# Down projection of an adaLN block: the first token pair with ten instead of eight pairs of K tiles in seven products

## Chip, core and metric

The kernel runs on one core of one Trainium2 chip. The metric is the device time of one execution in microseconds (us), the median of several runs. The engines of the core run side by side, each with its own queue of instructions, and wait for each other by semaphores: PE (TensorE, the matmuls), DVE (VectorE), ACT (ScalarE), POOL (GpSimd) and SP (SyncE, which issues nearly all DMAs here). K is the dimension that a matmul sums over; a K tile is 128 of it.

## What is computed

A transformer block of 2048 tokens and width 1024: a layer norm with modulation, linear attention, a second modulated layer norm, and a gated feed-forward network (FFN) of inner width 3584. The part that matters here is the last line of `_B_ref`, the product of the 2048 x 3584 gated values with `w_down`, and the residual sum around it.

```
def _B_ref(x, w_gate, w_up, w_down):
    return _gelu(x @ w_gate) * (x @ w_up) @ w_down
...
h = _layernorm(x, axis=-1) * (1 + cb) + sb
x = x + gb * _B_ref(h, B_w_gate, B_w_up, B_w_down)
return x
```

## The kernel before

**Stages.** Layer norm and attention take up to about 240 us. Then the FFN runs as 28 units (`unit`, L1514), 14 for each half of the tokens; a unit computes 256 of the 3584 gated values and stores them to DRAM (`y_store`, L1506) from one of three output tiles YS. From about 600 us the down projection runs, in eight token pairs of two chunks of 128 tokens. This change concerns the first of them, pair 0, which begins inside the last unit.

**Seven products.** The gate, up and down matrices are multiplied by the Strassen-Winograd scheme. For the down projection the two token chunks of a pair make two rows of blocks, the two halves of 512 output columns two columns of blocks, and two neighbouring K tiles the inner index. Eight block products become seven: P1 and P2 take the plain bf16 operands, P5, P6, P7, P3 and P4 take sums of blocks, held as fp32r. A product is one 128 x 128 by 128 x 512 matmul for each pair of K tiles (`d_prod`, L1667). The 28 K tiles make 14 such pairs, numbered j. Pairs 1 to 7 use all 14. Pair 0 uses the products for j = 0 to 7 (`NJP`, L67); its other twelve K tiles are multiplied plainly, twelve matmuls for each of its four output parts (`down`, L1603).

**Operands.** The weights come in seven loads of four K tiles, wd 0 to 6 (`wd_dma`, L1383), so load q serves j = 2q and 2q + 1. From each load `d_t` (L1620) makes five T operands: T0, T1, T2 on DVE, T3 a copy on ACT, and T4 on DVE, which overwrites the right half of the load itself, so that this half can no longer be used plainly. P5 uses S0 and T0, P6 S1 and T1, P7 S2 and T2, P3 S3 and T3, P4 S4 and T4. The S operands are sums of a pair's y blocks (`d_s`, L1647): S0 to S3 on DVE, S4 a copy on ACT, each in two halves, j = 0 to 6 and the rest. They share two buffers: S0, S2, S4 the one, S1, S3 the other, in alternation from pair to pair, so S2 can be written when P5 has read S0, and S3 when P6 has read S1.

**PSUM banks of pair 0.** P1 and P2 sum in bank 0. ACT copies P1 into bank 2 (`d_cp`), P6 adds to it, ACT copies that into bank 1, P7 and later P4 add to bank 2. P5 stands alone in bank 3; ACT copies it to the tile DE (`d_ecp`). DVE adds DE to bank 1 (`d_add(1, 1)`) and writes bank 2 plus DE into bank 3 (`d_add(3, 2)`). P3 adds to bank 1. The plain parts 0 to 3 add to banks 0, 1, 2 and 3.

**Order.** In this stage every engine's order is the program order of the Python code; nothing reorders it. `d_pair0` (L1716) issues the products and plain parts of pair 0; P1 was already issued by `d_first` inside the last unit, ahead of that unit's own product P4 (list at L1864). After each step `hook0` (L1874) issues other work: the T sums of the later loads, S sums, evacuations (`evac`, L1588, two DVE steps and a store), and reloads of y for pair 1 (`y_in`, L1584), which can only start where pair 0 has finished with the y it replaces. In this list a number k from 1 to 7 is product Pk, 0 is the plain part 0, and 11, 12, 13 are the plain parts 1, 2, 3.

**Memory.** Many tiles lie in memory that earlier ones have left. Each `OFF_DT` entry (L72) gives the places of T0 to T3 of a load. Load 4's T0 and T1 lie where an operand of the last unit's P4 lies, T2 where another operand of that P4 lies, and T3 lies in the output tile YS0, which the last unit stores. A tracker derives every wait from these places.

Of the kernel before, what the change touches and what calls it, by code (L numbers as in the profile page):

```python
# [33 lines left out]
OFF_HT = OFF_XALL + NCH * HP * 2  # L34
# [15 lines left out]
OFF_GAB = OFF_CONST  # L50
# [13 lines left out]
OFF_KVT = OFF_GUH + 2048  # L64
OFF_YS = [OFF_YT + 32768 + i * 4096 for i in range(3)]
NDJ = NFC // 2
NJP = (8,) + (NDJ,) * 7  # L67
NSJ = NDJ // 2
YRB = NDJ * 2 * P * 2
WDQ = [OFF_R3, OFF_R3 + 8192, OFF_R3 + 16384, OFF_WS, OFF_HT + 16384, OFF_WS + 8192, OFF_WS + 16384]  # L70
# [1 line left out]
OFF_DT = (tuple(OFF_XALL + i * 4096 for i in range(4)), tuple(OFF_XALL + i * 4096 for i in range(4, 8)),  # L72
          (OFF_HT, OFF_HT + 4096, OFF_GUH, OFF_GUH + 4096),
          (OFF_YS[1], OFF_TMP + 8192, OFF_TMP + 4096, OFF_YS[2]),
          (OFF_HT + 8192, OFF_HT + 12288, OFF_R3 + 24576, OFF_YS[0]),
          (OFF_GAB, OFF_ROW, OFF_YT, OFF_YT + 4096),
          tuple(OFF_YT + 16384 + i * 4096 for i in range(4)))
OFF_YA = (OFF_HT + 24576, OFF_YT + 45056)
OFF_SB = [(OFF_YT + 45056 + YRB, OFF_YT + 8192), (OFF_SMALL + 2048, OFF_YT + 8192 + NSJ * 512)]
# [251 lines left out]
def bass_adaLN_cond__linear_attn_block__geglu_ffn__prompt_kernel(  # L331
# [18 lines left out]
    with ExitStack() as es:  # L350
# [1032 lines left out]
        def wd_dma(q):  # L1383
            f0, f1 = 4 * q, 4 * q + 4
            sch.dma(Q, lambda e: e.dma_start(WDT[q][:], wd_v[:, f0:f1, :]), wr=[t_ for fc in range(f0, f1) for t_ in r_wd(fc)], note=f"wd{q}")
# [194 lines left out]
        def x_in(i, *ns):  # L1580
            for n in ns:
                sch.dma(Q, lambda e, n=n: e.dma_start(XQ[n][:], scr_x[:, 2 * i + n // 2, n % 2 * 512:n % 2 * 512 + 512]), wr=r_xq(n), deps=[x_st[i // 2]], note=f"xq{i}.{n}")

        def y_in(i, r, j0=0, j1=NDJ):  # L1584
            sch.dma(Q, lambda e: e.dma_start(YA[r][:, j0:j1, :], scr_y[2 * i + r, :, j0:j1, :]), wr=[(OFF_YA[r] + j0 * 512, OFF_YA[r] + j1 * 512, f"ya{r}")],
                    deps=[y_st[u] for u in range(i // CPG * NFP, (i // CPG + 1) * NFP)], note=f"{'ya' if j0 == 0 else 'yt'}{i}.{r}")

        def evac(c_, k, b, c0, c1):  # L1588
            n = 2 * (c_ % 2) + k
            sch.op(V, lambda e: e.tensor_tensor(PS(b), PS(b), GBB[:, c0:c1], ALU.mult), prd=pr(b), pwr=pr(b), rd=R_GBB, note=f"x2a c{c_}.{k}")  # L1590
            sch.op(V, lambda e: e.tensor_tensor(XQ[n][:, :], PS(b), XQ[n][:, :], ALU.add), prd=pr(b), rd=r_xq(n), wr=r_xq(n), note=f"x2b c{c_}.{k}")
            sch.dma(Q, lambda e: e.dma_start(out_v[:, c_, c0:c1], XQ[n][:, :]), rd=r_xq(n), note=f"out{c_}.{k}")
# [27 lines left out]
        def d_t(i, q):  # L1620
            j0, j1 = 0, 2
            w = WDT[q][:, 2 * j0:2 * j1, :].rearrange("p (j r) d -> p j r d", r=2)
            b = lambda r, cc: (w[:, :, r, cc * 512:(cc + 1) * 512], r_wh(q, r, cc, f"wd{q}", j0, j1))
            t32 = lambda k: (dt_ap(q, k, j0, j1)[0].bitcast(f32), dt_ap(q, k, j0, j1)[1])
            dst, wr = dt_ap(q, i, j0, j1)
            if i == 3:
                src, rd = b(1, 1)
                sch.op(A, lambda e: e.activation(dst, src, ACTF.Copy), rd=rd, wr=wr, note=f"dtcp {q}")
                return
            (in0, r0), (in1, r1) = ((b(0, 1), b(0, 0)), (b(1, 1), t32(0)), (b(1, 1), b(0, 1)), None, (b(1, 0), t32(1)))[i]  # L1630
            if i == 4:
                in0, in1 = (t_.rearrange("p j (h c) -> p j h c", h=2) for t_ in (in0, in1))
            sch.op(V, lambda e: e.tensor_tensor(dst, in0, in1, ALU.subtract), rd=r0 + r1, wr=wr, note=f"dtsum {q}.{i}")

        def nj(ca):
            return NJP[ca // 2]

# [9 lines left out]
        def d_s(ca, i, hs=(0, 1)):  # L1647
            cb, n = ca + 1, nj(ca)
            for j0, j1 in (((0, min(n, NSJ)), (NSJ, n))[h] for h in hs):
                if j0 >= j1:  # L1650
                    continue
                dst, wr = ds_ap(ca, i, j0, j1)
                if i == 4:
                    src, rd = y_ap(cb, 1, j0, j1)
                    sch.op(A, lambda e, dst=dst, src=src: e.activation(dst, src, ACTF.Copy), rd=rd, wr=wr, note=f"dscp {cb}")
                    continue
                s_ = lambda k: (ds_ap(ca, k, j0, j1)[0].bitcast(f32), ds_ap(ca, k, j0, j1)[1])
                (in0, r0), (in1, r1), op = ((y_ap(cb, 0, j0, j1), y_ap(cb, 1, j0, j1), ALU.add), (s_(0), y_ap(ca, 0, j0, j1), ALU.subtract),
                                            (y_ap(ca, 0, j0, j1), y_ap(cb, 0, j0, j1), ALU.subtract), (y_ap(ca, 1, j0, j1), s_(1), ALU.subtract))[i]
                sch.op(V, lambda e, dst=dst, in0=in0, in1=in1, op=op: e.tensor_tensor(dst, in0, in1, op), rd=r0 + r1, wr=wr, note=f"dssum{i} {cb}")  # L1660
# [39 lines left out]
        def parts_of(i):  # L1700
            return tuple((2 * i + n // 2, n % 2, i % 2 * 4 + n, n % 2 * 512, n % 2 * 512 + 512) for n in range(4))
# [4 lines left out]
        def d_add(dst, src):  # L1706
            sch.op(V, lambda e: e.tensor_tensor(PS(dst), PS(src), DE[:, :], ALU.add), prd=pr(src), rd=R_DE, pwr=pr(dst), note="dpadd")

        def d_ecp(b):
            sch.op(A, lambda e: e.activation(DE[:, :], PS(b), ACTF.Copy), prd=pr(b), wr=R_DE, note="descp")  # L1710
# [4 lines left out]

        def d_pair0(hook):  # L1716
            parts = parts_of(0)
            for k in (2, 6, 5, 0, 7, 3, 13, 11, 12, 4):
                n = k - 10 if k > 10 else k
                if k in (0, 11, 12, 13):  # L1720
                    down(*parts[n], list(range(2 * nj(0), NFC)), n != 2, True)
                    hook(k)
                    continue
                d_prod(0, 0, k)
                if k == 6:
                    d_cp(1, 2, "ducp")
                elif k == 5:
                    d_ecp(3)
                    d_add(1, 1)
                elif k == 7:  # L1730
                    d_add(3, 2)
                hook(k)
# [128 lines left out]
        for u in range(2 * NFP):  # L1861
            if u == 0:
                unit(u, ORD0)
            elif u == 2 * NFP - 1:  # L1864
                unit(u, (1, lambda: (d_t(0, 3), d_s(0, 0, (0,)), d_s(0, 1, (0,))), 2, lambda: (wd_dma(4), wd_dma(5)), 6, 5, 7,
                         lambda: (d_t(1, 3), d_s(0, 0, (1,)), d_s(0, 1, (1,))), 3, lambda: (wd_dma(6), x_in(0, 0, 1, 2, 3)), d_first, lambda: (d_t(2, 3), d_t(3, 3)), 4))
            else:
                a = ACTS.get(u, ((), ()))
                unit(u, (1, 2, lat(DMAS.get(u, nop), DVES.get(u, nop), *a[0]), 6, 5, lat(*a[1]), 7, 3, 4))
            if u == 1:  # L1870
                mark.append(sch.n)
        held[0]()
        held[0] = None
        def hook0(k):  # L1874
            if k == 2:
                d_t(0, 4)
            elif k == 6:
                d_s(0, 3)
                d_t(0, 5)
            elif k == 5:  # L1880
                d_s(0, 2)
                y_in(1, 0, 0, nj(0))
            elif k == 0:
                evac(*parts_of(0)[0])
            elif k == 7:
                d_s(0, 4)
                y_in(1, 1, 0, nj(0))
                d_t(4, 3)
                d_t(0, 6)
            elif k == 3:  # L1890
                d_t(1, 4)
                d_t(1, 5)
                d_t(3, 4)
            elif k == 13:
                d_t(1, 6)
                d_s(2, 0, (0,))
                d_t(3, 5)
            elif k == 11:
                d_t(2, 4)
                d_t(3, 6)  # L1900
            elif k == 12:
                for r in range(2):
                    y_in(1, r, nj(0), NDJ)
                evac(*parts_of(0)[3])
            elif k == 4:
                x_in(1, 0, 3)
                d_s(2, 1, (0,))
                d_s(2, 0, (1,))
                d_s(2, 1, (1,))

        def hooks(i):
            def hook(k):
                more = i + 1 < 2 * CPG
                if i == 1:
                    if k in (6, 2):
                        n = 1 if k == 6 else 2
                        evac(*parts_of(0)[n])
                        x_in(1, n)
                    if k in (6, 7, 2):
                        d_t(4, {6: 4, 7: 5, 2: 6}[k])  # L1920
                else:
                    if k == 5:
                        x_in(i, 1, 2)
                    if not more and k in (5, 6):
                        for q in {5: (0, 1), 6: (2,)}[k]:
                            t_gb(q)
                if more and k in (1, 4):
                    x_in(i + 1, 3 if k == 1 else 0)
            return hook
# [82 lines left out]
```

## Time and profile before

| | us |
|---|---|
| median of 3 runs | 782.14 (781.69 to 782.68) |
| profiled execution | 781.62 |
| its span, first to last instruction | 779.8 |
| PE busy in the span | 773.0 |
| DVE busy | 647.4 |
| ACT busy | 377.3 |
| first matmul of pair 0 starts at | 597.64 |
| opening product of pair 1 starts at | 622.60 |
| pair 1, opening products to opening products | 635.18 to 657.22 |
| pair 2, the same | 657.22 to 679.19 |

All times in the trace count from the span's first instruction. The granted clock of TensorE was 1.00 throughout. Matmuls overlap in the array, so the row of a group tells its pitch by the number in it, not by the length of one. In a row of the timeline the square brackets give how long the engine had been idle before it and what released it. The row of a DMA shows when SP issued it; its landing, when the semaphore tells that all of it has arrived, is a number of its own.

### The profile page before, as it was taken

To read this page: it belongs to the slowest core of one execution; us is meant where nothing else is said; L and a number is where in the kernel's file an instruction comes from. 1 tells how busy PE (TensorE), PEld (TensorE's weight loads), DVE (VectorE), ACT (ScalarE), POOL (GpSimd) and SP (SyncE) were. 2 spreads that over 40 slices of the span, in tenths; PEclk is the share of its full clock that TensorE was granted. 3 is DMA by queue.
4 is the path that set the end of the run, shared out by engine and by line. 5 is a ranking of instruction groups with operands and counts; after the bars stand their busy time and mean duration, and the time that the engine had idled before them with its cause. 6 is when DMAs were issued, how large, how long until landed. Compare 5 with 4: busy or idle time off the path is not lost.

```text
span 779.8 us, 10832 instructions
## 1 busy us (share of the span) xinstructions
PE 773.0 (99%) x3883; PEld 496.9 (64%) x3883; DVE 647.4 (83%) x970; ACT 377.3 (48%) x635; POOL 49.2 (6%) x126
## 2 busy tenths in 40 slices
PE   8999999999999999999999999999999999999998
PEld 4444445666445667767676767667676567777766
DVE  6699988897898878787989888898989888667668
ACT  2497743242484487877755555555555211101111
POOL 2031300000331011100000000000000000000000
PEclk9999999999999999999999999999999999999999
DMA  9789749949996258967353865535357334443341
GB/s 290 250 169 251 157 94 221 258 125 203 209 271 182 82 147 204 237 169 215 104 140 110 261 203 168 149 96 162 98 146 223 111 123 142 137 148 98 132 143 54
DMA packets 196940, 130.22 MB, mean 167 GB/s; under 512 B 69516, under 2 KB 182420, under 8 KB 195864
## 3 DMA queue, kind: packets, MB, share of 16 engines
q1 hardware_dynamic: 196872, 129.55, 62.2%
q8 instruction: 30, 0.49, 0.3%
q14 instruction: 22, 0.18, 0.1%
q10 hardware_dynamic: 16, 0.00, 0.0%
HBM read 92.55 MB, written 23.35 MB: 149 GB/s over the span
## 4 chain that ended last, share of the span: by engine, by line
PE 96%; SPq 2%; DMA 1%; DVE 0%; issue 0%; DVEq 0%
PE ps_all L1472 45%; PE ps_all L1684 21%; PE ps_all L895 7%; PE ps_all L1292 7%; PE ps_all L934 7%; PE ps_all L880 6%; PE ps_all L1607 1%; SPq L598 1%; DMA wmq<-in_w_mod_dram 1%; SPq L603 1%; PE ps_all L913 0%; PE ps_all L1203 0%; PE ps_all L1246 0%; SPq L592 0%; PE ps_all L766 0%; PE ps_all L840 0%
## 5 line engine op out<-in xcount | busy, mean ns | idle before, releaser
L1472 PE MATMUL ps_all<-ss,tp 128*128 128x512 f32 x896 | 214.3, 396 | 0.0
L1472 PEld LDWEIGHTS ps_all<-ss,tp 128*128 128x128 f32 x896 | 168.2, 188 | 37.8 <-DVE ss L1427 0.3
L1472 PE MATMUL ps_all<-h2a,wt 128*128 128x512 bf16 x448 | 101.6, 380 | 0.0
L1684 PE MATMUL ps_all<-dt,sb 128*128 128x512 f32 x424 | 101.1, 394 | 0.0
L1495 ACT ACTIVATE ge<-ps_all 128x512 f32<-128x512 f32 x112 | 64.2, 597 | 73.8 <-DVE ps_all L1483 62.1
L1684 PEld LDWEIGHTS ps_all<-dt,sb 128*128 128x128 f32 x424 | 79.5, 188 | 17.9 <-DVE sb L1660 0.5
L1490 DVE TENSOR_TENSOR ps_all<-ps_all,es 128x512 f32<-128x512 f32 x54 | 37.6, 699 | 49.6 <-ACT es L1480 49.3
L1502 DVE TENSOR_TENSOR ys<-ge,ps_all 128x512 bf16<-128x512 f32 x112 | 74.5, 684 | 3.4 <-PE ps_all L1684 0.5
L1472 PEld LDWEIGHTS ps_all<-h2a,wt 128*128 128x128 bf16 x448 | 37.9, 97 | 57.3 <-ACT ps_all L1477 17.0
L1447 DVE TENSOR_TENSOR tp<-wt,tp 128x1024 fp32r<-128x1024 bf16 x56 | 68.3, 1220 | 0.0
L1447 DVE TENSOR_TENSOR tp<-wt 128x1024 fp32r<-128x1024 bf16 x56 | 68.2, 1218 | 0.0
L880 PE MATMUL ps_all<-wk,h1T 128*128 128x512 bf16 x248 | 56.8, 379 | 0.5 <-DVE h1T L724 0.5
L934 PE MATMUL ps_all<-h1T,wq 128*128 128x512 bf16 x256 | 56.7, 379 | 0.0
L1292 PE MATMUL ps_all<-w,pq 128*128 128x512 bf16 x256 | 56.4, 379 | 0.0
L1472 PE MATMUL ps_all<-ar,tp 128*128 128x512 f32 x224 | 55.5, 390 | 0.0
L869 ACT ACTIVATE eb<-ps_all 128x512 f32<-128x512 f32 x64 | 36.5, 595 | 38.2 <-PE ps_all L880 16.3
L1710 ACT ACTIVATE de<-ps_all 128x512 f32<-128x512 f32 x14 | 8.4, 599 | 90.2 <-PE ps_all L1684 90.2
L1684 PE MATMUL ps_all<-wd,ya 128*128 128x512 bf16 x212 | 47.7, 380 | 0.0
L1472 PEld LDWEIGHTS ps_all<-ar,tp 128*128 128x128 f32 x224 | 42.0, 188 | 8.8
L1477 ACT ACTIVATE ps_all<-ps_all 128x512 f32<-128x512 f32 x56 | 32.6, 583 | 30.7 <-PE ps_all L1472 30.7
L934 PEld LDWEIGHTS ps_all<-h1T,wq 128*128 128x128 bf16 x256 | 25.0, 98 | 30.0
L1292 PEld LDWEIGHTS ps_all<-w,pq 128*128 128x128 bf16 x256 | 24.7, 98 | 30.2 <-issue 1.1
(141 smaller groups left out, 992.2 us busy)
## 6 DMA issues: line engine op xcount, KB each, us to landing
wt<-in_B_w_gate_dram SPq DMA_DIRECT2D x28, 512.0 KB, 4.0
wt<-in_B_w_up_dram SPq DMA_DIRECT2D x28, 512.0 KB, 5.2
scr_y<-ys SPq DMA_DIRECT2D x28, 512.0 KB, 3.2
ya<-scr_y SPq DMA_DIRECT2D x14, 896.0 KB, 5.0
rb<-scr_rd SPq DMA_DIRECT2D x32, 256.0 KB, 6.4
wd<-in_B_w_down_dram SPq DMA_DIRECT2D x7, 1024.0 KB, 7.3
wmst<-in_w_mod_dram SPq DMA_DIRECT2D x6, 1024.0 KB, 5.8
wmq<-in_w_mod_dram SPq DMA_DIRECT2D x8, 512.0 KB, 6.9
```

Source lines behind the costliest of these rows:

```text
L869: sch.op(A, lambda e: e.activation(EB[i][:, :], PS(bank), ACTF.Exp), prd=pr(bank), wr=rng, note=f"{note}.exp")
L880: o = sch.op(T, lambda e, dc=dc: e.matmul(PS(bank), H1[sg][:, ci, dc, :], W_[:, dc, jg * 512:(jg + 1) * 512], start=(dc == 0), stop=(dc == ...
L895: o = sch.op(T, lambda e, c_=c_: e.matmul(PS(bank, 0, n), PK[c_][:, g * P:(g + 1) * P], xrow(c_, o_, o_ + n), start=(c_ == 0), stop=(c_ == ...
L934: o = sch.op(T, lambda e, dc=dc: e.matmul(PS(b), WQ[:, dc, qc * P:(qc + 1) * P], H1[sg][:, :, dc, :], start=(dc == 0), stop=(dc == NDC - 1 ...
L1292: last[half] = sch.op(T, lambda e, g=g, half=half: e.matmul(PS(b0 + half), PQ[sg][:, g, ci * P:(ci + 1) * P], W2[:, g, half * 512:(half + ...
L1447: sch.op(V, lambda e: e.tensor_tensor(TP[k][:], in0, in1 if k in (0, 2) else in1[:], ALU.subtract), rd=r0 + r1, wr=r_tp(k), deps=[x1_ops[7 ...
L1472: o = sch.op(T, lambda e, l_=l_, r_=r_, dc=dc: e.matmul(PS(b), l_, r_, start=fresh and dc == 0, stop=dc == ND2 - 1, skip_group_check=True) ...
L1477: sch.op(A, lambda e: e.activation(PS(BB + t), PS(BA + t), ACTF.Copy), prd=pr(BA + t), pwr=pr(BB + t), note="pcp")
L1490: sch.op(V, lambda e: e.tensor_tensor(PS(BC + t), PS(BC + t), ES[t][:, :], ALU.add), prd=pr(BC + t), rd=r_2k(OFF_ES[t], f"es{t}"), pwr=pr( ...
L1495: sch.op(A, lambda e: e.activation(GE[i][:, :], PS(b), ACTF.Gelu_apprx_tanh), prd=pr(b), wr=r_2k(OFF_GE[i], f"ge{i}"), note="gelu")
L1502: sch.op(V, lambda e: e.tensor_tensor(YS[s_][:, 2 * h:2 * h + 2, t, :], q(GE[i][:, :]), q(PS(b + 1)), ALU.mult), rd=r_2k(OFF_GE[i], f"ge{i ...
L1684: o = sch.op(T, lambda e, l_=l_, r_=r_, j=j, dst=dst: e.matmul(dst, l_[:, 0, :], r_, start=(k in (1, 5) or k == 7 and 0 < ca < 4 * CPG - 2 ...
```

## The change

Pair 0 takes ten pairs of K tiles in seven products and eight K tiles plainly. Product P5 goes ahead of P6. For this the five T operands of load 4 are made earlier: T0 inside the last unit, ahead of its last output product; T1 and T3 behind P2; T2 behind P5; T4, which was made in pair 1, behind P7. S2 is now issued ahead of S3, S3 behind part 0's matmuls, and the first two sums of loads 5 and 6 move back by one step. T0 and T1 of load 4 now lie where an operand of the last unit's P5 lay, and T2 and T3 of load 5 take their old places.

```
-NJP = (8,) + (NDJ,) * 7
+NJP = (10,) + (NDJ,) * 7
...
-          (OFF_HT + 8192, OFF_HT + 12288, OFF_R3 + 24576, OFF_YS[0]),
-          (OFF_GAB, OFF_ROW, OFF_YT, OFF_YT + 4096),
+          (OFF_YT, OFF_YT + 4096, OFF_R3 + 24576, OFF_YS[0]),
+          (OFF_GAB, OFF_ROW, OFF_HT + 8192, OFF_HT + 12288),
...
         def d_pair0(hook):
-            for k in (2, 6, 5, 0, 7, 3, 13, 11, 12, 4):
+            for k in (2, 5, 6, 0, 7, 3, 13, 11, 12, 4):
...
                 d_prod(0, 0, k)
-                if k == 6:
+                if k == 5:
+                    d_ecp(3)
+                elif k == 6:
                     d_cp(1, 2, "ducp")
-                elif k == 5:
-                    d_ecp(3)
+                    hook(k)
                     d_add(1, 1)
+                    continue
...
             elif u == 2 * NFP - 1:
-                         ... d_first, lambda: (d_t(2, 3), d_t(3, 3)), 4))
+                         ... d_first, lambda: (d_t(2, 3), d_t(3, 3), d_t(0, 4)), 4))
...
         def hook0(k):
             if k == 2:
-                d_t(0, 4)
-            elif k == 6:
-                d_s(0, 3)
-                d_t(0, 5)
+                d_t(1, 4)
+                d_t(3, 4)
             elif k == 5:
                 d_s(0, 2)
+                d_t(2, 4)
+            elif k == 6:
                 y_in(1, 0, 0, nj(0))
             elif k == 0:
+                d_s(0, 3)
                 evac(*parts_of(0)[0])
             elif k == 7:
                 d_s(0, 4)
                 y_in(1, 1, 0, nj(0))
                 d_t(4, 3)
+                d_t(4, 4)
+                d_t(0, 5)
+            elif k == 3:
                 d_t(0, 6)
-            elif k == 3:
-                d_t(1, 4)
                 d_t(1, 5)
-                d_t(3, 4)
             elif k == 13:
                 d_t(1, 6)
                 d_s(2, 0, (0,))
                 d_t(3, 5)
             elif k == 11:
-                d_t(2, 4)
                 d_t(3, 6)
...
         def hooks(i):
-                    if k in (6, 7, 2):
-                        d_t(4, {6: 4, 7: 5, 2: 6}[k])
+                    if k in (7, 2):
+                        d_t(4, {7: 5, 2: 6}[k])
```

More of the change, by code (lines that the diff above doesn't have):

```diff
@@ L1865, in bass_adaLN_cond__linear_attn_block__geglu_ffn__prompt_kernel @@
                 unit(u, (1, lambda: (d_t(0, 3), d_s(0, 0, (0,)), d_s(0, 1, (0,))), 2, lambda: (wd_dma(4), wd_dma(5)), 6, 5, 7,
-                         lambda: (d_t(1, 3), d_s(0, 0, (1,)), d_s(0, 1, (1,))), 3, lambda: (wd_dma(6), x_in(0, 0, 1, 2, 3)), d_first, lambda: (d_t(2, 3), d_t(3, 3)), 4))
+                         lambda: (d_t(1, 3), d_s(0, 0, (1,)), d_s(0, 1, (1,))), 3, lambda: (wd_dma(6), x_in(0, 0, 1, 2, 3)), d_first, lambda: (d_t(2, 3), d_t(3, 3), d_t(0, 4)), 4))
             else:
```

## Prediction

> **What bounds the kernel now.** I read the page first: how busy the engines are and the chain of waits that ended last.
>
> ```profile
> span 779.8 us, 10832 instructions
> ...
> PE 773.0 (99%) x3883; PEld 496.9 (64%) x3883; DVE 647.4 (83%) x970; ACT 377.3 (48%) x635; POOL 49.2 (6%) x126
> ...
> PE 96%; SPq 2%; DMA 1%; DVE 0%; issue 0%; DVEq 0%
> ```
>
> TensorE is the bound from end to end. A change gains only by issuing fewer or shorter matmuls, or by removing a stall of PE; it loses only where it makes PE wait. So I need the pitch of the two kinds of matmul, and PE's present stalls. The timeline of a later, undisturbed pair gives the pitch (columns: start, length, engine, line, operation, count).
>
> ```profile
> 657.22 6.22 PE L1684 MATMUL ps_all<-wd,ya 128*128 128x512 bf16 x28
> ...
> 663.08 3.57 PE L1684 MATMUL ps_all<-dt,sb 128*128 128x512 f32 x14
> ...
> 679.19 6.22 PE L1684 MATMUL ps_all<-wd,ya 128*128 128x512 bf16 x28
> ```
>
> A single matmul is shown as 0.38 us long, but they are pipelined: 28 plain ones take 6.22, so the pitch is (6.22 - 0.38)/27 = **0.2163 us**. From 657.22 to 679.19 lie 28 of these and 70 sum products (f32 operands): (21.97 - 28 x 0.2163)/70 = **0.2274 us**. A sum product costs 0.011 us more than a plain one. Next, PE's timeline over the first pair.
>
> ```profile
> 597.64 1.90 PE L1684 MATMUL ps_all<-wd,ya 128*128 128x512 bf16 x8
> 599.19 2.19 PE L1472 MATMUL ps_all<-ar,tp 128*128 128x512 f32 x8
> 601.22 1.90 PE L1684 MATMUL ps_all<-wd,ya 128*128 128x512 bf16 x8
> 602.77 4.00 PE L1684 MATMUL ps_all<-dt,sb 128*128 128x512 f32 x16
> 606.61 2.76 PE L1607 MATMUL ps_all<-wd,ya 128*128 128x512 bf16 x12
> 609.18 3.93 PE L1684 MATMUL ps_all<-dt,sb 128*128 128x512 f32 x16
> 612.95 7.94 PE L1607 MATMUL ps_all<-wd,ya 128*128 128x512 bf16 x36
> 620.54 2.21 PE L1684 MATMUL ps_all<-dh,sb 128*128 128x512 f32 x8
> 622.60 3.19 PE L1684 MATMUL ps_all<-wd,ya 128*128 128x512 bf16 x14
> ```
>
> From the first product (597.64) to pair 1's opening product (622.60) are 24.96 us. In it are 16 + 48 = 64 plain and 40 + 8 sum matmuls (8 belong to the last FFN unit): 64 x 0.2163 + 48 x 0.2274 = 24.76. So only 0.20 is stall. Stretch by stretch: 606.61 to 612.95 is 6.34 against 12 x 0.2163 + 16 x 0.2274 = 6.23, a stall of 0.10; the other three stretches lose 0.02 to 0.04 each, 0.10 together, at the changes of kind. The 0.10 is P7's wait for S2, named by the weight load's row, first below.
>
> ```profile
> 609.18 3.50 PEld L1684 LDWEIGHTS ps_all<-dt,sb 128*128 128x128 f32 x16 [0.30 <-DVE sb L1660]
> ...
> 647.56 2.59 PEld L1684 LDWEIGHTS ps_all<-dt,sb 128*128 128x128 f32 x12 [0.19 <-DVE sb L1660]
> ```
>
> The second is pair 2's S0, late behind pair 1's sums on DVE. It costs 0.07: pair 1, from 635.18 to 657.22, lasts 22.04 against the next pair's 21.97.
>
> **The change, part by part.**
>
> *PE's work.* Seven products over ten pairs of K tiles are 70 matmuls (20 plain, 50 sum), where there were 56 (16, 40); four parts over eight K tiles are 32, where there were 48. 104 become 102. Plain 64 to 52 saves 12 x 0.2163 = 2.60, sum 40 to 50 costs 10 x 0.2274 = 2.27: **-0.32 us**. That is the whole certain gain: each pair of K tiles moved swaps 8 plain matmuls for 7, five of them dearer.
>
> *The new course of PE*, by these pitches from 597.64: P1 to 599.80, the unit's P4 to 601.62, P2 to 603.78, P5 to 606.06, P6 to 608.33, part 0 to 610.06, P7 to 612.34, P3 to 614.61, three parts to 619.80, P4 to 622.08. Against it I lay each operand's arrival.
>
> *Third S-sums.* The second halves of S0 and S1 cover three j instead of one. DVE rows: 1.09 us for 896 columns, 0.28 for 128; by the line between them 384 columns take 0.55, so +0.27 each. The output product behind them (599.35) and all that follows on DVE slip by 0.54. Nothing on PE waits for these: S0 is first used at 603.78. Cost 0.
>
> *Fifth load's sums.* T0 of load 4 now stands on DVE ahead of the last output product: 599.94 + 0.54 is T2 of load 3, one step of 1.14 later (sums follow at 1.14: 3.49 for three) T0 runs 601.62 to 602.84; P5 wants it at its ninth matmul, 605.6. Its operand, load 4, was issued at 590.55 and lands 6.6 us later (597.1), also ahead of P1's ninth matmul (599.4). T1 runs from about 603.4 to 604.6, P6 wants it at 607.9. S2's first half starts when P5 has read that half of S0, near 605.6; S2 is done by 607.2; T2 by 608.4, wanted by P7 at 611.9. S2's first half is there three microseconds before P7 at 610.06: **the 0.10 stall goes**. Cost 0 as long as DVE keeps this lead.
>
> *The output store and the scalar copy.* This is the one new wait. T3 of load 4 (a copy on ACT, in the buffer of the last output tile) moves from behind P3 to right behind P2, and has to wait until the last store of that tile has landed. Behind it on ACT stand P5's copy to DE and the copy of bank 2 to bank 1; P7 may not add to bank 2 before that copy, and DVE's sum in bank 1 waits for it. The page's DMA issues, SP's timeline and the DMA issues of that one moment give the last store: issued 602.41 and 4.9 us to landing, where the median of the 28 stores is 3.2.
>
> ```profile
> scr_y<-ys SPq DMA_DIRECT2D x28, 512.0 KB, 3.2
> ...
> 602.41 0.37 SPq L1508 DMA_DIRECT2D scr_y<-ys  x1
> ...
> scr_y<-ys SPq DMA_DIRECT2D x1, 512.0 KB, 4.9
> ```
>
> After the change the output product is not at 601.64 but behind T0, at 602.76, so the store is issued near 603.53. With 3.2 it lands at 606.7, with 4.9 at 608.4. T3 then takes 1.05, the copy to DE 0.60, the copy of the bank 0.58 (rows of 600.07, 606.81, 604.99), some 0.1 overlapped each: bank 2 is free 2.2 us after landing, at 608.9 but not before P6 has ended (608.5) plus 0.6, so 609.15; or at 610.6. P7 is due at 610.06. So the cost lies between **0 and +0.55**. I take 0, since the 4.9 row shared the DMA engines with load 6 and four residual loads issued at 597.88 to 599.97, whose queue will have drained 1.1 us further when the store starts.
>
> The Trainium skill, page "DMA: Bandwidth & Descriptors", section on the anatomy of one DMA, fits a transfer (one that GpSimd issues) as 2.0 us plus its bytes over 436 GB/s: for this store an estimate of 3.2 us, which the median row matches and the 4.9 row doesn't. By the rule the sum stays as it is, by that row it gives back 0.55.
>
> *Reloads of y.* SP's order is kept. The first reload (640 KB instead of 512) is freed by S2 at 607.2 instead of 609.39; the second by S4 and S3, near 614.1 instead of 612.41, and with the 3.6 us of its row lands near 618. DVE uses them for pair 1's S0 only at 620.2. The tails (256 KB instead of 384) go after the last plain part, 620.05 and 620.45 instead of 620.76 and 621.17; at the 3.4 us of their row they land by 623.9. The opening product wants its eleventh pair at 622.08 + 10 x 0.2163 = 624.2. Cost 0.
>
> *DVE to the end of the pair.* Bank 1's sum at 609.2, S3 to 611.4 (P3 at 612.34), evacuation of part 0 to 612.8, bank 3's sum to 613.5 (its plain part at 614.61), then six T-sums to 620.2 where there were five sums, of which one is T4 of load 4, brought forward from pair 1. Pair 1's S0 is complete by 624.9, wanted at 625.1 (first half, done 621.2) and 626.7. With T4 gone from pair 1, its DVE work ends 1.1 us sooner and the 0.07 wait of pair 2 goes: **-0.07**.
>
> **Sum**: -0.32 - 0.10 - 0.07 = -0.49. The profiled execution goes from its 779.8 (781.62 with what lies around the span) to 779.3; the median of the runs shown, 782.14, to **781.65**.
>
> **Rivals.**
>
> *B, the store eats the gain.* It again takes 4.9 us, P7 waits 0.55, and the sum is +0.06: 782.2. For it: the same load 6 and residual loads go ahead of the store. Against it: the shortest and the median of the 28 stores are both 3.2, and what was ahead has 1.1 us more.
> Here the order on ACT decides: in this trace T3 of load 4 ran only at 612.23, behind S4's copy, which itself waited 3.76 for PE, although its buffer was free at 607.3. The Trainium skill, "TensorE: Matmul & The Clock Gate", section "Architectural detail", says that ScalarE's queue is strictly in order; the trace agrees.
>
> *C, slower: the queue on ACT.* The same copy as in B, but with a store so late that P7 stands still. From a landing at about 607.9 each microsecond goes into P7's start; from 608.4 (4.9 after issue) the whole is slower than before. The far row is load 5 with 8.6 us to landing: 612.1, bank 2 free at 614.3, P7 4.2 late, net +3.7: 785.9. Against it: that was 1 MB, and behind another.
>
> *D, the trade yields half on PE.* If sum matmuls ran at the spacing that half the saving needs, (2.60 - 0.16)/10 = 0.244, for example with DVE and PE contending, only -0.33 would be left: 781.8. The undisturbed pairs speak against it.
>
> **Numbers.** Forecast 0.66, B 0.23, C 0.05, D 0.06. A measurement of this kernel tells about 0.2% (1.56 us) from no change; forecast, B and D all lie inside. Their extremes are 781.65 and 782.2; the runs shown scatter by -0.45 and +0.54 about their median, so the range is 780.9 to 782.8, with C outside. Slower 0.05; faster 0.03, since no more than 0.49 can be found in PE; within, 0.92.
>
> **What would show it.** The line of seven products: 432, 108 and 216 matmuls instead of 424, 106 and 212; the plain line 32 instead of 48. Pair 1's opening product at 622.2 instead of 622.60. No wait of DVE's S-sums ahead of P7, nor at pair 2. The copy of bank 2 (ACT, line of 604.99) ending before 610.0; if P7 starts late and that copy is its releaser, B or C. I am wrong altogether if PE stalls over 0.3 us anywhere from 597 to 660.

## The result and the profile after

| | before | changed |
|---|---|---|
| median of 22 runs each, us | 782.34 (781.57 to 784.58) | 781.52 (780.37 to 782.60) |
| ratio, 95% interval | | 0.9986 (0.9980 to 0.9993) |
| the same kernels, two later comparisons (11 runs of the changed one each) | | 0.9998 (0.9989 to 1.0007), 0.9993 (0.9984 to 1.0002) |
| profiled span, us | 779.8 | 779.7 |
| pair 0's first product to pair 1's opening product | 24.96 | 24.51 |
| pair 0's first product to pair 2's P2 | 59.58 | 59.09 |

The median is 781.52 where 781.65 was forecast. The change gains a little, and less than one comparison of this kernel can size: the three ratios mean gains of 1.1, 0.2 and 0.5 us. The trace sizes it better. From pair 0's first product to pair 2's P2 it shows -0.49 us, and the two later traces of the changed kernel give 59.09 again. A later pair runs P5, P6, P7, P2, the next pair's P1, P3, P4; so each row of 28 plain matmuls, as those at 635.18 and 657.22 before, is a pair's P2 and then the next pair's opening product, and the start of pair 2's P2 is what the expectation of ten_again below calls pair 2's opening. The two spans differ by only 0.1 because the start of pair 0, ahead of which nothing was changed, fell at 597.64 before and at 598.15 in the changed kernel's profile; in its later traces it fell at 597.77 and 597.99.

The page of the changed kernel: span, busy time, and the two groups of its products with sums and its plain products.

```profile
span 779.7 us, 10826 instructions
...
PE 773.1 (99%) x3881; PEld 498.7 (64%) x3881; DVE 648.1 (83%) x970; ACT 377.0 (48%) x635; POOL 49.7 (6%) x126
...
PE 96%; SPq 2%; DMA 1%; DVE 0%; issue 0%; DVEq 0%
...
L1684 PE MATMUL ps_all<-dt,sb 128*128 128x512 f32 x432 | 103.0, 394 | 0.0
...
L1684 PE MATMUL ps_all<-wd,ya 128*128 128x512 bf16 x216 | 48.4, 380 | 0.0
```

Two matmuls fewer (x3883 to x3881), and the counts 432 and 216. PE is the bound as before. Its timeline over pair 0, in the same columns as before:

```profile
598.15 2.33 PE L1684 MATMUL ps_all<-wd,ya 128*128 128x512 bf16 x10
600.13 2.18 PE L1472 MATMUL ps_all<-ar,tp 128*128 128x512 f32 x8
602.15 2.33 PE L1684 MATMUL ps_all<-wd,ya 128*128 128x512 bf16 x10
604.13 4.90 PE L1684 MATMUL ps_all<-dt,sb 128*128 128x512 f32 x20
608.87 1.90 PE L1607 MATMUL ps_all<-wd,ya 128*128 128x512 bf16 x8
610.42 4.91 PE L1684 MATMUL ps_all<-dt,sb 128*128 128x512 f32 x20
615.17 5.35 PE L1607 MATMUL ps_all<-wd,ya 128*128 128x512 bf16 x24
620.17 2.64 PE L1684 MATMUL ps_all<-dh,sb 128*128 128x512 f32 x10
622.66 3.19 PE L1684 MATMUL ps_all<-wd,ya 128*128 128x512 bf16 x14
```

52 plain and 58 sum matmuls at the pitches 0.2163 and 0.2274 make 24.44; the stretch is 24.51, so 0.07 of stall is left where there was 0.20. The weight loads ahead of P7 and of pair 2's P5, which reads S0, no longer wait for DVE.

```profile
610.39 4.51 PEld L1684 LDWEIGHTS ps_all<-dt,sb 128*128 128x128 f32 x20
...
647.49 9.48 PEld L1684 LDWEIGHTS ps_all<-dt,sb 128*128 128x128 f32 x42
```

ACT's timeline shows the one new wait:

```profile
607.96 1.06 ACT L1628 ACTIVATE dt<-wd 128x1024 fp32r<-128x1024 bf16 x1 [5.41 <-DMA scr_y<-ys]
608.92 0.58 ACT L1710 ACTIVATE de<-ps_all 128x512 f32<-128x512 f32 x1
609.40 0.59 ACT L1704 ACTIVATE ps_all<-ps_all 128x512 f32<-128x512 f32 x1
```

ACT stands 5.41 us for the last store, then makes T3 of load 4 and the two bank copies. The second ends at 609.99, and P7 starts at 610.42: 0.43 us to spare. So the question for the experiments is what covered the trade and what this wait would cost.

### The profile page after: what moved, and what is told of

It is laid out like the page before. It is cut to its first block, busy times and chain, and to the rows that moved or that the text cites. A ratio compares the mean times of both kernels' runs of the same rounds, so it can differ in the third digit from the quotient of the medians.

```text
span 779.7 us, 10826 instructions
## 1 busy us (share of the span) xinstructions
PE 773.1 (99%) x3881; PEld 498.7 (64%) x3881; DVE 648.1 (83%) x970; ACT 377.0 (48%) x635; POOL 49.7 (6%) x126
## 4 chain that ended last, share of the span: by engine, by line
PE 96%; SPq 2%; DMA 1%; DVE 0%; issue 0%; DVEq 0%
PE ps_all L1472 45%; PE ps_all L1684 22%; PE ps_all L895 7%; PE ps_all L1292 7%; PE ps_all L934 7%; PE ps_all L880 6%; SPq L598 1%; DMA wmq<-in_w_mod_dram 1%; PE ps_all L1607 1%; SPq L603 1%; PE ps_all L913 0%; PE ps_all L1203 0%; PE ps_all L1246 0%; SPq L592 0%; PE ps_all L840 0%
## 5 line engine op out<-in xcount | busy, mean ns | idle before, releaser
L1684 PE MATMUL ps_all<-dt,sb 128*128 128x512 f32 x432 | 103.0, 394 | 0.0
L1684 PEld LDWEIGHTS ps_all<-dt,sb 128*128 128x128 f32 x432 | 81.2, 188 | 17.9
```

The source lines that it names most:

```text
L1684: o = sch.op(T, lambda e, l_=l_, r_=r_, j=j, dst=dst: e.matmul(dst, l_[:, 0, :], r_, start=(k in (1, 5) or k == 7 and 0 < ca < 4 * CPG - 2 ...
```

## The experiments

In some of these traces the first matmul record of a group of plain ones is missing. So the table measures from the end of the last FFN unit's P3 (0.2274, one pitch, after its last matmul starts) to the start of pair 1's first sum product, whose record all have, and from there to the start of the last matmul. Times in us, each from one profiled execution.

| kernel | pair 0 | to the last matmul | ratio of the runs, where timed |
|---|---|---|---|
| before | 27.81 | 150.99 | |
| changed, three traces | 27.35 | 150.80 | above |
| order_only | 28.50 | 150.90 | 1.0008 (0.9998 to 1.0018) |
| s2_first | 27.75 | 150.85 | 1.0001 (0.9992 to 1.0010) |
| order_copy_behind | 27.75 | 150.83 | |
| copy_behind | 27.35 | 150.81 | |
| store_sooner | 27.35 | 150.81 | |
| store_later | 27.57 | 150.80 | |
| two_more_copies | 29.14 | 150.81 | |
| twelve_pairs | 27.36 | 151.02 | 0.9990 (0.9981 to 0.9999) |
| unit_first | 27.08 | 151.48 | 0.9998 (0.9989 to 1.0007) |
| unit_first_2 | 27.11 | 151.33 | 0.9987 (0.9978 to 0.9996) |

**The order alone.** The changed kernel with eight pairs:

```
-NJP = (10,) + (NDJ,) * 7
+NJP = (8,) + (NDJ,) * 7
...
             elif k == 7:
-                d_t(4, 4)
...
-                    if k in (7, 2):
-                        d_t(4, {7: 5, 2: 6}[k])
+                    if k in (6, 7, 2):
+                        d_t(4, {6: 4, 7: 5, 2: 6}[k])
```

> The change's order and its early sums of load 4, but eight pairs of K tiles in products and twelve K tiles plain as before (T4 of load 4 stays in pair 1). Theory, the gain is the trade of matmuls (-0.32 us) plus two short waits: from pair 0's first product to pair 1's opening product 24.86 us (before 24.96, changed 24.51), the wait ahead of P7 gone, time 0.1 to 0.2 us under before. Rival, the order brings the gain: 24.5 to 24.6 us and a time like the changed kernel's, 0.5 to 1.1 us under before.

Neither came true: the stretch grew to 25.65, 0.70 longer than before. ACT's and PE's rows say where.

```profile
607.78 1.06 ACT L1628 ACTIVATE dt<-wd 128x1024 fp32r<-128x1024 bf16 x1 [6.03 <-DMA scr_y<-ys]
608.74 0.58 ACT L1710 ACTIVATE de<-ps_all 128x512 f32<-128x512 f32 x1
609.22 0.59 ACT L1704 ACTIVATE ps_all<-ps_all 128x512 f32<-128x512 f32 x1
```

```profile
606.75 2.76 PE L1607 MATMUL ps_all<-wd,ya 128*128 128x512 bf16 x12
609.95 3.88 PE L1684 MATMUL ps_all<-dt,sb 128*128 128x512 f32 x16 [0.44 <-ACT ps_all L1704]
```

P7 waited for ACT's copy of bank 2, which ended at 609.81, and started at 609.95, 12.17 us after pair 0's first product (597.78). In the next kernel, where nothing holds it up, it starts 11.39 after it, 0.78 sooner. The store landed 4.6 us after its issue here. Behind P7 another weight load, at 613.79, waited 0.39 for DVE's sum in bank 3, which had slipped with it. This is the forecast's rival B, in a kernel with less cover: with ten pairs P7 starts 12.27 us after pair 0's first product (610.42 less 598.15). Those 0.88 us, the longer products ahead of P7, are what the changed kernel gives ACT; by the count of matmuls they are 0.91.

**The same with the copy out of the way.** In that kernel T3 of load 4 goes behind the copy of bank 2 on ACT:

```
             if k == 2:
                 d_t(1, 4)
-                d_t(3, 4)
...
             elif k == 6:
                 y_in(1, 0, 0, nj(0))
+                d_t(3, 4)
```

> The kernel with the change's order and eight pairs (order_only), with T3 of load 4 moved on ACT behind the copy of bank 2. Theory, order_only lost its 0.70 us only to ACT's wait for the last store: without it the stretch from pair 0's first product to pair 1's first sum product is 27.7 us (before 27.80, order_only 28.50), and the copy stands well ahead of P7. Rival, DVE's order (S3 behind part 0, the sum in bank 3 late) cost a part of it: 28.0 to 28.5 us.

```profile
609.08 4.03 PE L1684 MATMUL ps_all<-dt,sb 128*128 128x512 f32 x16
```

Measured 27.75, as the theory said: moving one copy gives back 0.76 us, all that order_only lost and 0.06 more. DVE's order cost nothing by itself. Against copy_behind below (27.35), in which T3 stands in the same place, this also isolates the trade of matmuls, ten pairs against eight in nearly the same order (T4 of load 4 stands elsewhere): -0.39, of which 0.32 is the count of matmuls by their pitch. The other 0.07 is spread in bits of 0.01 to 0.03 over the stretches and is not settled.

**S2 first, in the kernel before.** The one edit lets S2 go to DVE ahead of the sum in bank 1:

```
                 elif k == 5:
                     d_ecp(3)
+                    hook(k)
                     d_add(1, 1)
+                    continue
```

> The kernel before with one edit: S2 is issued on DVE ahead of the sum in bank 1, which waits for the copy to DE. Theory, P7's wait in the kernel before came from DVE's order, not from PE's: S2 is done near 608.2 and the stretch to pair 1's opening product falls from 24.96 to 24.86 us, with no other change. Rival, P7 waits for S2 because P5 comes late behind P6: the wait stays and the stretch stays 24.96 us.

```profile
609.24 2.72 PEld L1684 LDWEIGHTS ps_all<-dt,sb 128*128 128x128 f32 x12
```

The weight load ahead of P7 no longer waits for S2, and the stretch falls from 24.96 to 24.90: the direction of the theory, 0.06 of the 0.10. So P7's old wait came from DVE's order and not from P6 standing ahead of P5; order_copy_behind, in which P5 does go first, has the same 24.90. The other 0.04 is not explained. The run times can't tell a thing of this size.

**How much ACT can bear.** First the changed kernel with `d_t(3, 4)` written three times in `hook0`, k == 2.

> The changed kernel with the copy T3 of load 4 made three times, so that two more copies of 0.95 us stand on ACT between the landing of the last store and the copies of the banks. Theory, ACT's order is the only new tight place and its lead ahead of P7 is 0.4 us (the copy of bank 2 ended at 609.99, P7 started at 610.42): P7 starts 1.5 us late and the stretch from pair 0's first product to pair 1's opening product is 26.0 us instead of 24.51. Rival, the copies hide behind PE's queue or behind part 0's plain matmuls: 24.5 us.

```profile
607.45 3.24 ACT L1628 ACTIVATE dt<-wd 128x1024 fp32r<-128x1024 bf16 x3 [5.41 <-DMA scr_y<-ys]
610.60 0.58 ACT L1710 ACTIVATE de<-ps_all 128x512 f32<-128x512 f32 x1
611.08 0.59 ACT L1704 ACTIVATE ps_all<-ps_all 128x512 f32<-128x512 f32 x1
```

```profile
608.36 1.90 PE L1607 MATMUL ps_all<-wd,ya 128*128 128x512 bf16 x7
611.81 4.57 PE L1684 MATMUL ps_all<-dt,sb 128*128 128x512 f32 x19 [1.54 <-ACT ps_all L1704]
```

The three copies, which write the same place, took 3.24, so each further one 1.09 and not the 0.95 of copies to different places: 2.18 more. The stretch grew by 1.79, so 0.39 was hidden: the lead read from the trace (0.43). The theory holds, its number was low by the longer copies. What went past that lead, PE lost.

Then the opposite: in the changed kernel the copy T3 goes behind the copy of bank 2, with the edit of order_copy_behind.

> The changed kernel with T3 of load 4 issued on ACT behind the copy of bank 2, so that nothing ahead of P7 waits for the store. Theory, the lead of the bank's copy over P7 grows from 0.4 to over 0.9 us, and PE's stretch stays 24.5 us, since the wait cost nothing. Rival, the store's wait does cost PE: the stretch falls below 24.4 us.

27.35, unchanged. The bank's copy ended at 609.56 for a P7 at 610.33, a lead of 0.77 rather than over 0.9, since it is then P6's end that sets it. In the changed kernel the wait for the store costs nothing, but by a margin of only 0.4 us.

**When the store is issued.** T0 of load 4 behind the last output product:

```
-  ... d_first, lambda: (d_t(2, 3), d_t(3, 3), d_t(0, 4)), 4))
+  ... d_first, lambda: (d_t(2, 3), d_t(3, 3)), 4))
...
             if k == 2:
+                d_t(0, 4)
                 d_t(1, 4)
```

> The changed kernel with T0 of load 4 behind the last output product on DVE instead of ahead of it, so that the last store is issued some 0.7 us sooner. Theory, all but one of the 16 parts of the store land 3.2 us after the issue and a 16 KB load of instructions holds up one engine's part by 0.6 to 1.0 us: landing 3.2 to 4.9 us after the issue, depending on where that load falls. PE's stretch stays 24.5 us, for T0 is still there for P5's ninth matmul. Rival, the landing is set by the queue of loads ahead and stays where it was, near 9.7 us after pair 0's first product.

and T1, too, ahead of it (`d_t(1, 4)` moved from k == 2 into the list above):

> The changed kernel with T1 of load 4, too, ahead of the last output product, so that the store is issued 1.1 us later (near 605.1 in the changed kernel's times). Theory, landing 3.2 to 3.9 us after that, 608.3 to 609.0, then T3 and two copies in 2.1 us: the copy of bank 2 ends at 610.4 to 611.1 and P7, due at 610.4, starts 0 to 0.8 us late; stretch 24.5 to 25.3 us. Rival, ACT's wait for the store isn't what sets P7: 24.5 us whatever the landing.

Issued 5.20 us after pair 0's first product the store landed 4.5 us later, at 9.7; in the changed kernel 5.87 and 3.8, again 9.7; in the late one 7.11 and 3.2, at 10.3. So issuing it 0.7 sooner gained nothing, as the rival had it. The landing events of the trace show why: in store_sooner 15 of the 16 parts come 3.55 after the issue and the last 0.91 later, in the changed kernel 3.19 and 0.64. So of the 0.63 us that the landing took longer, 0.36 lies in the 15 parts and 0.27 in the last. The first fits the rival's reason, loads still ahead in the queue, for the sooner the issue, the longer the 15 took: 3.85 us with an issue 4.77 after pair 0's first product in the kernel before, 3.55 at 5.20, 3.42 at 5.33 in order_only, 3.19 at 5.87, 3.17 at 7.11. The late store cost 0.21 us, within the expected 0 to 0.8: its bank copy ended at 610.97, 12.43 after pair 0's first product, where P7 had been due at 12.27.

**Further along.** Twelve pairs, with all sums of load 5 ahead of their products:

```
-NJP = (10,) + (NDJ,) * 7
+NJP = (12,) + (NDJ,) * 7
...
             if k == 2:
+                d_t(0, 5)
                 d_t(1, 4)
+                d_t(3, 5)
                 d_t(3, 4)
             elif k == 5:
+                d_t(1, 5)
                 d_s(0, 2)
                 d_t(2, 4)
             elif k == 6:
                 y_in(1, 0, 0, nj(0))
+                d_t(2, 5)
...
```

> One step further: twelve pairs of K tiles in products, four K tiles plain, all sums of load 5 but none of load 6 ahead of their products. Theory, each pair of K tiles moved saves 8 x 0.2163 - (2 x 0.2163 + 5 x 0.2274) = 0.161 us on PE: the stretch to pair 1's opening product falls from 24.51 by 0.32 to 24.2 us, as P7 now follows P6 after only four plain matmuls and may wait up to 0.1 us for the copy of bank 2. Time 0.3 us under the changed kernel. Rival, the sums and copies no longer fit: PE waits at P7, P3 or pair 1's P5 by more than 0.32 us in all, stretch over 24.5, no gain over ten pairs.

The stretch was 24.51: no gain over ten, the rival's number. The weight loads' row of the first wait, and ACT's row of the copy that P7 needs:

```profile
600.44 0.11 PEld L1684 LDWEIGHTS ps_all<-wd,ya 128*128 128x128 bf16 x2 [0.45 <-DMA wd<-in_B_w_down_dram]
```

```profile
611.02 0.58 ACT L1704 ACTIVATE ps_all<-ps_all 128x512 f32<-128x512 f32 x1 [1.05 <-PE ps_all L1684]
```

P1's eleventh matmul waits for load 5; that part of the stretch (598.15 to 602.73) is 0.17 over its pitch. In unit_first below, where nothing holds it up, P7 starts 0.67 after part 0's first matmul; here that would be 611.50, but the copy ends at 611.60 and P7 starts at 611.75. That part (610.83 to 617.29) is 0.14 over. Together they eat the 0.32.

If so, an order in which neither wait can arise should win it back. In unit_first the last unit's P4 goes ahead of P1, and pair 0 runs in another order:

```
-            for k in (2, 5, 6, 0, 7, 3, 13, 11, 12, 4):
+            for k in (5, 6, 2, 0, 7, 3, 13, 11, 12, 4):
...
-  ... 3, lambda: (wd_dma(6), x_in(0, 0, 1, 2, 3)), d_first, lambda: (d_t(2, 3), d_t(3, 3), d_t(0, 4)), 4))
+  ... 3, lambda: (wd_dma(6), x_in(0, 0, 1, 2, 3)), 4))
...
+        for i_, q_ in ((3, 3), (3, 5), (0, 4), (0, 5), (1, 3)):
+            d_t(i_, q_)
+        d_s(0, 1, (1,))
+        d_t(1, 4)
+        d_first()
...
```

The sums in `hook0` move with it.

> Twelve pairs of K tiles again, but the last unit's P4 goes ahead of pair 0's P1, and pair 0 runs P1, P5, P6, P2, plain part 0, P7, P3 and so on: P1 comes later than load 5's landing, P5 stands between P1 and its copy, P2 covers the copy of bank 2 that P7 waits for, and T3 of load 4 stands on ACT behind that copy. Theory, twelve pairs lost their 0.32 us to P1's wait for load 5 (0.45 us on the weight loads) and to P7's wait for bank 2, nothing else: from the end of the last unit's P3 to pair 1's first sum product 27.0 to 27.1 us (before 27.80, ten pairs 27.35, twelve pairs 27.36). Rival, DVE can't make the sums of loads 4 and 5 in time for P5 and P6 (it is busy without a break until P7): PE waits at P6, P7 or P3, 27.4 us or more.

Pair 0 took 27.08, as the theory said: from P2 to the plain parts (608.41 to 617.35) 16 plain and 24 sum matmuls took 8.94 against 8.92 by pitch, so P7's wait is gone. But 0.67 was lost afterwards: the opening product of pair 2 waited for a reload of y.

```profile
639.06 2.71 PEld L1684 LDWEIGHTS ps_all<-wd,ya 128*128 128x128 bf16 x14 [1.02 <-DMA ya<-scr_y]
```

That reload was issued at 632.97, against 630.95 in the changed kernel, and landed 6.0 us later: 15 of its parts by 637.28, one at 639.02. It took both to make the wait. The changed kernel's own reload lands 6.0 to 6.2 us after its issue in its three traces, the last part 1.6 to 1.8 behind the others, but issued 2 us sooner it is in time; and in unit_first the 15 parts were there before the product was due (635.33 + 14 x 0.2163 = 638.36). The last kernel lets S2 go sooner:

```
             elif k == 7:
-                evac(*parts_of(0)[0])
                 d_s(0, 4)
                 y_in(1, 1, 0, nj(0))
+                evac(*parts_of(0)[0])
...
-        d_t(2, 6)
...
+                    if k == 5:
+                        d_t(2, 6)
```

> unit_first with two moves: SP issues the second reload of y for pair 1 ahead of the store of part 0's evacuation again (it was stuck behind it, 617.67), and T2 of load 6 goes behind pair 1's S2 on DVE. Theory: unit_first won its 0.28 us in pair 0 (27.07 us from the end of the last unit's P3 to pair 1's first sum product, ten pairs 27.35) and lost 0.70 in pair 1, where the opening product of pair 2 waited for a reload of y that S2 had let go only at 632.97. With S2 sooner by some 2 us that wait goes: 27.1 us again, and from there to the last matmul 150.8 us as with ten pairs (unit_first 151.5); a ratio to before near 0.9990. Rival, the reload lands late for another reason, for example what else the DMA engines carry: 151.2 us or more again.

Pair 0 again 27.11, the reload was issued at 629.49, and pair 2 did not wait. The rest was still 151.33 and not 150.8, the rival's number, though not at pair 2: in this trace the opening product of pair 6, in code that all versions share, came 0.52 late for its reload:

```profile
725.79 1.19 PEld L1684 LDWEIGHTS ps_all<-wd,ya 128*128 128x128 bf16 x7 [0.86 <-DMA ya<-scr_y]
```

In the trace of twelve_pairs the same product lost 0.21 us. In both SP issued this reload, behind loads of the residual, 1.1 us later than in the changed kernel, counted from pair 5's P2; what held SP up is not settled. In the kernel before it was pair 7's opening product, which lost 0.14. The three traces of the changed kernel have none of this. Timed, unit_first_2 is faster than before (0.9987, 0.9978 to 0.9996). Its interval overlaps those of the changed kernel; by the traces it gains 0.25 us more in pair 0.

**The changed kernel again.**

> The changed kernel once more, for its time and its trace beside the other kernels on the same chip. Theory: 24.5 us from pair 0's first product to pair 1's opening product and 59.1 us to pair 2's opening again; the code ahead of pair 0 is the same, so where its first product starts (597.64 before, 598.15 changed) varies by some 0.5 us from run to run and explains what the two profiled spans don't show of the gain. Rival: the start of pair 0 is always later in the changed kernel, by 0.5 us, and the gain of the runs comes from elsewhere.

> The changed kernel a third time, beside unit_first on one chip. Theory: 27.35 us from pair 0's first product to pair 1's first sum product as in both traces so far, and a ratio to the kernel before near 0.9994 (0.49 us of 782), so that the 0.9986 of the first comparison was larger than the change by scatter. Rival: 0.9986 again, a gain of 1.1 us of which the traces show less than half.

Both traces repeat 24.51 and 59.09 to 0.01 us. Pair 0 began at 597.77 and 597.99, so the late start of the first profile was scatter. The ratios, 0.9998 and 0.9993, lie on both sides of 0.9994; 0.9986 was not repeated.

## Why the prediction was right

*The trade.* -0.32 from the count of matmuls by two pitches; isolated by two kernels in nearly the same order (order_copy_behind and copy_behind), -0.39. The rival D, a costlier pitch of the added sum products, is out: from 602.15 to 608.87 the ten of P2 and the twenty of P5 and P6 take 6.72, against 6.71 by the old pitches.

*P7's wait for S2.* Put at 0.10; removing it alone in the kernel before gave 0.06. It was DVE's order. That P5 now precedes P6 had no part in it, as s2_first keeps the old order of products.

*Pair 2's wait.* Put at 0.07: pair 1's 22.04 went to 21.97, as forecast. order_copy_behind, in which T4 of load 4 stays in pair 1, keeps 0.05 of it.

*The sum.* -0.49 forecast and -0.49 in the trace to pair 2's P2. That it meets to 0.01 is luck: the terms came as -0.39 for -0.32, -0.06 for -0.10 and -0.07 for -0.07, and pair 1's first 42 sum products take 0.02 longer (9.76 against 9.74), which the forecast put at nothing and no run explains. Their mechanisms are the forecast ones, their errors cancel. The 781.65 against the measured 781.52 is closer than these runs can resolve, and luck too: the median that it starts from, 782.14, was 782.34 in the later runs, and the ratio of 0.9986 means more than twice the gain in the trace. The low end of the range, 780.9, doesn't follow from the working, which gives 781.65 - 0.45 = 781.2; the median lies inside both. Behind pair 2 the trace of before has a late reload (0.14) which is not the change's doing.

*The store and ACT's order.* Here the prediction named the right place and took the cost as 0 between 0 and 0.55. The landing came between its two rows, 3.8 us after an issue at 604.02. Its ground, that the loads ahead would have drained, fits 15 of the 16 parts: they came 3.19 after the issue where they took 3.85 before. The Trainium skill's fit on the page "DMA: Bandwidth & Descriptors", in the section on the anatomy of one DMA, gives an estimate of 3.2 us; the changed kernel's 15 parts (3.19) and the whole of store_later's store (3.18) agree with it, the changed kernel's last part (3.83) doesn't. The lead over P7 was 0.43; by the prediction's own course it would have been 0.58, since that has P7 due 12.42 after pair 0's first product (610.06 less 597.64) and the trace 12.27. What the prediction did not see is that this cover comes from the change itself: with eight pairs the same order loses 0.7 us against the kernel before. The product count and the order were costed as separate terms, and the second is only free with the first.

*Rival C.* In the traces of kernels in which ACT waits for the store it landed 3.2 to 4.6 us after its issue, in the kernel before 4.9; the longest, 6.2 and 7.6, were in unit_first and unit_first_2, issued sooner behind the last loads, where nothing waited for it. C's price is confirmed: two_more_copies put 2.18 us into that queue and PE lost 1.79.

## What to carry to other kernels

Count the stalls of the bounding engine in one stage against pitch times count before believing in a gain; here 0.20 of 24.96 us was all there was besides the matmuls. A copy that waits for a DMA at the head of an engine's queue delays all that stands behind it, and costs what the bounding engine's own work doesn't cover: read that lead from the trace in microseconds, and move the copy behind the others if its reader can wait. Where the gain is below the scatter of the runs, the same stretch in several traces tells more than the times: it repeated to 0.01 us while the medians moved by 0.5.

## What the runs showed of the hardware

A DMA's landing here is set by its slowest sixteenth: ACT's copy started at 607.96, behind the last part (607.85) and not behind the other 15 (607.21). In the changed kernel 15 parts of the last store landed within 0.2 us of each other, the last 0.6 later; in the kernel before the last was 1.05 late, in store_sooner 0.9, in store_later not at all. In the changed kernel the DMA rows of the microsecond from 604 to 605, in which the store was issued, show one load of instructions on a queue of its own, a packet of 16 KB:

```profile
q1 hardware_dynamic: 169, 0.14, 41.1%
q8 instruction: 1, 0.02, 6.2%
...
scr_y<-ys SPq DMA_DIRECT2D x1, 512.0 KB, 3.8
```

It started at 604.57. In the kernel before, its like started at 604.12 and took 0.99 us, about what the store's last part was late; in store_later it started at 605.08, ahead of the store's issue at 605.66, and no part was late. A 16 KB packet at 746.18 in the kernel before stands likewise between 15 parts of pair 7's reload (by 746.32) and its last (748.26). The fourteen traces of this case together say it more firmly; they hold the landing events of 280 stores of y. In 25 of these such a packet started 0.1 to 2.1 us behind the issue, and each had its last part 0.5 to 2.1 us behind the other 15. In 236 none started between issue and landing, and no last part was more than 0.44 late. (In the other 19 it started 2.9 us or more behind the issue; 18 of them had last parts up to 0.35 late, one 1.57.) That such a packet holds up the DMA engine that carries the late part is still argued from these times, not tried. Some parts are later than one packet took, as the 1.9 us of pair 7's reload; and in the changed kernel a packet at 746.08 stands beside the same reload with the last part only 0.35 late.
